# Spreading two blocks' head outputs to partitions: one set of four 64-column products at the end in place of two sets of 32

## The chip, the cores and the metric

The kernel runs on one core of a Trainium2 chip. The metric is the device time of one execution in microseconds (us), as the median of several runs; each profile is one further execution. All runs quoted here are fast: none is over 1.5% above the fastest run of its kernel. The "granted clock" is the share of PE's full clock that the trace shows as granted to it. "PE" is the matrix engine, "PEld" its weight loads, "DVE" the vector engine, "ACT" the scalar engine, "SP" the engine that issues most DMA transfers.

## The reference

Two independent attention layers decode one token each; their two output rows of 512 are concatenated.

```python
# block A: 32 heads, 32768 keys each, head size 128
q = (x @ wq).reshape(heads)
p = softmax(q @ k_cache.T * 128 ** -0.5)
a = concat_heads(p @ v_cache) @ wo          # wo: 4096 x 512
# block B: 32 query heads, 8 key/value heads, only the last 4096 keys
b = ...same...                               # own x, wq, caches, wo
return concatenate([a, b])
```

Block A reads 32 x (8.39 MB of K + 8.39 MB of V) in bf16; block B reads 16.8 MB of caches, and each block has a `wq` and a `wo` of 4.19 MB. Everything is read once.

## The kernel before

Block B runs first, in straight code; then a loop over block A's 32 heads; then both output projections. SP issues each load as soon as PE has finished with the buffer (`self.free`): there are three K buffers of 4.19 MB, of which a head of A uses two, and one V buffer of 8.39 MB. The weight `wo` of each block comes last, A's in six pieces of falling size, so that little work remains behind the last one.

```python
    def plan(self):
        ...
            self.emit_PV("B", g)
        self.emit_spread("B")                      # <- the change touches this
        for g in range(NQH):                       # NQH = 32 heads of A
            self.load_k(g, 1 if 0 < g < NQH - 1 else 2)
            self.load_v(g)
            ...
        for n in ("B", "A"):
            for part in range(len(self.WO_CUTS[n]) - 1):
                self.load_wo(n, part)              # A: rows 0:11, 11:19, 19:25, 25:29, 29:31, 31:32
        self.emit_spread("A")                      # <- and this
        self.emit_proj()                           # B's 32 products, then A's, piece by piece
```

At the end of a block its head outputs lie in tile `G` of PSUM (the memory that PE writes its products to) as 32 rows (heads) by 128 columns, with the softmax sum beside them. The projection needs them with the 4096 values spread over 128 partitions, 32 columns each. Four small products with a 0/1 matrix (`spread`) do that:

```python
    def emit_spread(self, name):
        p2 = self.G[:, 448:480] if name == "B" else self.T[0]
        ri = self.op("dve", lambda v: v.reciprocal(t["rinv"][:, :], ps[0:32, DH:DH + 1]), self.gath)
        ob = self.op("dve", lambda v: v.tensor_scalar_mul(t["ob"][:, :], ps[0:32, 0:DH], t["rinv"][:, :]), ri)
        def mm(e):
            for dq in range(4):
                inst = e.matmul(p2[:, 0:32], lhsT=self.spread[:, 128 * dq:128 * dq + 128],
                                rhs=t["ob"][:, 32 * dq:32 * dq + 32], start=(dq == 0), stop=(dq == 3), ...)
            return inst
        o = self.op("pe", mm, ob, self.k_sel)
        t["ozop"] = self.op("dve", lambda v: v.tensor_copy(t["oz"][:, :], p2[:, 0:32]), o)   # the cast
    def proj_part(self, name, part, out):
        ...
        deps = (self.wosem[name][part], 16), self.c[name]["ozop"]    # weight piece landed, cast done
        return self.op("pe", mm, *deps)
```

Of the kernel before, what the change touches and what calls it, by code (L numbers as in the profile page):

```python
# [3 lines left out]
BF16 = mybir.dt.bfloat16  # L4
# [5 lines left out]
DH = 128  # L10
# [43 lines left out]
class _Kernel:  # L54
# [120 lines left out]
    def emit(self, eng):  # L175
# [22 lines left out]
        def body(e):  # L198
# [17 lines left out]
            for k, it in enumerate(need):  # L216
                cur, plan = {}, []
                for n in it:
                    w = []
                    for name, (sem, val) in n.items():  # L220
                        if name not in sems:
                            continue
                        rel = val - start[name] - step[name] * k
                        if rel > cur.get(name, 0):
                            cur[name] = rel
                            w.append((name, rel))
                    plan.append(sorted(w))
                plans.append(plan)
# [40 lines left out]
    def alloc(self):  # L269
        nc = self.nc  # L270
        sb = nc.alloc_sbuf_tensor
        self.kbuf = sb("kbuf", [128, 3 * HALF * DH], BF16, align_bytes=4096)
        self.vbuf = sb("vbuf", [128, 2 * HALF * DH], BF16, align_bytes=4096)
        self.kt = [sb(f"kt{i}", [128, 1024], BF16) for i in range(NKT)]
        self.psb = sb("psb", [128, 512], BF16)
        self.ptsb = sb("ptsb", [128, 512], BF16)
        self.ident = sb("ident", [128, 128], BF16)
        self.ones = sb("ones", [128, 128], BF16)
        self.e32 = sb("e32", [128, 32], F32)
        self.spread = sb("spread", [32, 4 * 129], BF16)  # L280
        self.tr = {k: sb(f"tr_{k}", [128, 32], F32) for k in ("in", "a")}
        self.rows64 = sb("rows64", [128, 64], F32)
        self.nscale = sb("nscale", [1, 128], F32)
        self.m4 = sb("m4", [1, 128], F32)
        self.out_sb = sb("out_sb", [1, 512], BF16)
        self.c = {}
        for name, d in self.X.items():
            HG = d["HG"]
            self.c[name] = dict(
                x=sb(f"x_{name}", [128, 12], BF16),  # L290
                oc=[sb(f"oc_{name}{i}", [128, DH + 1], F32) for i in range(2 if name == "B" else 1)],
                b=sb(f"b_{name}", [128, 32], F32),
                cm=sb(f"cm_{name}", [128, 32], F32),
                mr=sb(f"mr_{name}", [1, HG], F32),
                nb=sb(f"nb_{name}", [128, 2], F32),
                hot=sb(f"hot_{name}", [128, d["nb"]], F32),
                lh=sb(f"lh_{name}", [128, HG], F32),
                hsel=sb(f"hsel_{name}", [128, 64], F32),
                rinv=sb(f"rinv_{name}", [32, 1], F32),
                ob=sb(f"ob_{name}", [32, DH], BF16),  # L300
                oz=sb(f"oz_{name}", [128, 32], BF16),
            )

        self.qz = sb("qz", [128, 32 * self.X["B"]["NKVH"] + 64], BF16)
        self.qa = sb("qa", [128, NQH], BF16)
        self.qrow = sb("qrow", [128, 512], BF16)
        self.qw = sb("qw", [128, 64], BF16)
        self.hw = sb("hw", [128, 32], F32)
        ps = nc.alloc_psum_tensor
        self.S = ps("psS", [128, 512], F32)  # L310
        self.T = [ps(f"psT{i}", [128, 512], F32) for i in range(NT)]
        self.PT = ps("psPT", [128, 512], F32)
        self.ACC = ps("psACC", [128, 512], F32)
        self.G = ps("psG", [128, 512], F32)
        s = nc.alloc_semaphore
        self.ksem = [s(f"ksem{i}") for i in range(2)]
        self.vsem = [s(f"vsem{i}") for i in range(2)]
        self.xsem = {n: s(f"xsem_{n}") for n in self.X}
        self.wosem = {n: [s(f"wosem_{n}{i}") for i in range(len(self.WO_CUTS[n]) - 1)] for n in self.X}
        self.outsem = {n: s(f"outsem_{n}") for n in self.X}  # L320
# [72 lines left out]
    def plan(self):  # L393
        self.lsem = {"k": self.ksem, "v": self.vsem}
        self.fill = {w: [0, 0] for w in "kv"}
        self.free = {"k": [None] * 3, "v": [None] * 2}
        self.nbatch = 0
        self.copies = []
        self.pending = []
        self.psread = self.ptread = self.sread = self.accread = None  # L400
        self.gath = self.qcopy = self.hcopy = self.qread = None
        self.constants()
        a, b = self.X["A"], self.X["B"]

        self.load_wq("B")
        self.load_b("k", 0)
        self.load_wq("A")
        self.load_b("k", 1)
        self.emit_qproj("B")
        self.emit_unit("B", 0)  # L410
        self.emit_qproj("A")
        self.emit_stats("B", 0)
        self.emit_unit("B", 1, {1: lambda: self.emit_PT("B", 0)})
        self.emit_stats("B", 1)
        for g in range(2):
            if g == 1:
                self.emit_PT("B", g)
            self.load_b("v", g)
            self.emit_PV("B", g)
        self.emit_spread("B")  # L420

        for g in range(NQH):
            self.loop = {"pe": g, "dve": g // 2}
            self.load_k(g, 1 if 0 < g < NQH - 1 else 2)
            self.load_v(g)
            self.emit_qcopy(g)
            self.emit_unit("A", g)
            self.emit_stats("A", g)
            self.emit_PT("A", g)
            self.emit_PV("A", g)  # L430
        self.loop = {}
        for n in ("B", "A"):
            for part in range(len(self.WO_CUTS[n]) - 1):
                self.load_wo(n, part)
        self.emit_spread("A")
        self.emit_proj()

    def constants(self):
# [244 lines left out]
            self.G[0:32, c0 + c:c0 + c2], lhsT=win, rhs=t["oc"][g % len(t["oc"])][:, c:c2], start=False, stop=True,  # L683
            skip_group_check=True), *(self.accread, self.sread, self.hcopy if name == "A" else self.k_sel), to="dve")

    def emit_spread(self, name):

        t = self.c[name]
        c0 = self.GCOL[name]
        ps = self.G[:, c0:c0 + DH + 1]  # L690
        p2 = self.G[:, 448:480] if name == "B" else self.T[0]
        ri = self.op("dve", lambda v: v.reciprocal(t["rinv"][:, :], ps[0:32, DH:DH + 1]), self.gath)
        ob = self.op("dve", lambda v: v.tensor_scalar_mul(t["ob"][:, :], ps[0:32, 0:DH], t["rinv"][:, :]), ri)
        def mm(e):
            inst = None
            for dq in range(4):
                inst = e.matmul(p2[:, 0:32], lhsT=self.spread[:, 128 * dq:128 * dq + 128], rhs=t["ob"][:, 32 * dq:32 * dq + 32],
                                start=(dq == 0), stop=(dq == 3), skip_group_check=True)
            return inst
        o = self.op("pe", mm, ob, self.k_sel)  # L700
        t["ozop"] = self.op("dve", lambda v: v.tensor_copy(t["oz"][:, :], p2[:, 0:32]), o)

    def proj_part(self, name, part, out):

        a0, a1 = self.WO_CUTS[name][part:part + 2]
        oz, wo = self.c[name]["oz"], self.kbuf[:, HALF * DH * self.wo_third(name):]
        def mm(e):
            inst = None
            for a in range(a0, a1):
                inst = out(e, oz[:, a:a + 1], wo[:, 512 * a:512 * a + 512], a) or inst  # L710
            return inst
        deps = (self.wosem[name][part], 16), self.c[name]["ozop"]
        return self.op("pe", mm, *deps)

    def halves(self, e, bank, lhsT, rhs, begin, end, only=(0, 1)):
# [31 lines left out]
    def emit_proj(self):  # L747

        for part in range(2):
            o = self.emit_proj_b(part)  # L750
        o = self.sum_strips(o)
        self.op("sp", lambda e: e.dma_start(self.out[0, :, 512:1024], self.qrow[0:1, :]).then_inc(self.outsem["B"], 16), o)
        for part in range(len(self.WO_CUTS["A"]) - 1):
            self.proj_part("A", part, lambda e, lhsT, rhs, a: self.halves(e, self.PT, lhsT, rhs, a == 0, False)
                           if a < 31 else None)
        oz, wo = self.c["A"]["oz"], self.kbuf[:, HALF * DH * self.wo_third("A"):]
        done = []
        for i in range(2):
            o = self.op("pe", lambda e, i=i: self.halves(e, self.PT, oz[:, 31:32], wo[:, 512 * 31:512 * 32], False, True, (i,)),
                        (self.wosem["A"][-1], 16), self.c["A"]["ozop"])  # L760
            done.append(self.store(self.PT, i, o))
        self.op("sp", lambda e: e.dma_start(self.out[0, :, 0:512], self.out_sb[:, :]).then_inc(self.outsem["A"], 16), *done)

# [26 lines left out]
```

## Time and profile before

| | before |
|---|---|
| time, median of the first 3 runs | 1322.05 us (1322.04 to 1322.24) |
| span of the profiled run | 1320.8 us |
| moved by DMA | 570.59 MB, 432 GB/s over the span |
| PE, DVE busy | 73%, 57% |
| PE's waits for the next K load | 154.2 us in 31 waits |

These lines of the page give the span, the engines' busy time and share, the DMA engines' busy share in 40 slices (9 is 90% or more), and the packets, MB and share of two DMA queues.

```profile
span 1320.8 us, 28798 instructions
...
PE 968.0 (73%) x13248; PEld 677.4 (51%) x13248; DVE 753.3 (57%) x1342; ACT 56.4 (4%) x170; POOL 2.7 (0%) x22
...
DMA  9999999999999999999999999999999999999998
...
q1 hardware_dynamic: 13060, 570.43, 99.9%
q8 instruction: 8, 0.13, 0.0%
```

The DMA row has no slice under 9 before the last, and queue 1, which carries caches and weights, fills 99.9% of the engines' time. The kernel is therefore as long as its bytes take, plus a start and a tail. The Trainium skill's page "DMA: Bandwidth & Descriptors", section "Specifications", states 435 GB/s as the fabric ceiling into SBUF; the windows view of this trace has 434 GB/s over 170 to 600 us and over 600 to 1100 us, which agrees. Queue 8 carries instructions: 8 packets.

The two places that the change touches, in the timeline: start us, length us, engine, line, operation, output<-inputs, shape, count, and in brackets how long the engine had been idle and what ended that. First the gap between the blocks:

```profile
69.44 0.15 DVE L692 RECIPROCAL rinv_B<-psG 32x1 f32<-32x1 f32 x1 [0.50 <-PE psG L682]
69.63 0.34 DVE L693 TENSOR_SCALAR ob_B<-psG,rinv_B 32x128 bf16<-32x128 f32 x1
...
70.03 0.26 PE L697 MATMUL psG<-ob_B,spread 32*128 32x32 bf16 x4 [0.62 <-DVE ob_B L693]
70.32 0.19 DVE L701 CAST oz_B<-psG 128x32 bf16<-128x32 f32 x1 [0.35 <-PE psG L697]
...
72.48 1.78 PE L552 MATMUL psT<-ident,kbuf 128*128 128x128 bf16 x15 [2.19 <-DMA kbuf<-in_A_k_cache_dram]
```

B's four products take 0.26 us on PE (line 697), its cast 0.19 us on DVE (line 701), and PE then has nothing to do until A's first K half lands: 2.19 us idle before the transposes of head 0 at 72.48.

Second, the end:

```profile
1310.51 0.34 DVE L693 TENSOR_SCALAR ob_A<-psG,rinv_A 32x128 bf16<-32x128 f32 x1
...
1311.06 0.25 PE L697 MATMUL psT<-ob_A,spread 32*128 32x32 bf16 x4 [0.78 <-DVE ob_A L693]
...
1311.24 1.90 PE L730 MATMUL psS<-kbuf,oz_B 128*1 128x512 bf16 x32
1311.35 0.19 DVE L701 CAST oz_A<-psT 128x32 bf16<-128x32 f32 x1 [0.50 <-PE psT L697]
...
1312.97 1.37 PE L718 MATMUL psPT<-kbuf,oz_A 128*1 128x256 bf16 x22
...
1314.82 1.04 PE L718 MATMUL psPT<-kbuf,oz_A 128*1 128x256 bf16 x16 [0.48 <-DMA kbuf<-in_A_wo_dram]
...
1316.67 0.32 SPq L752 DMA_DIRECT2D out_dram<-qrow  x1
...
1316.73 0.82 PE L718 MATMUL psPT<-kbuf,oz_A 128*1 128x256 bf16 x12 [0.87 <-DMA kbuf<-in_A_wo_dram]
...
1317.97 1.21 PE L718 MATMUL psPT<-kbuf,oz_A 128*1 128x256 bf16 x14 [0.42 <-DMA kbuf<-in_A_wo_dram]
...
1319.20 0.41 DVE L725 CAST out_sb<-psPT 1x256 bf16<-1x256 f32 x1 [2.56 <-PE psPT L718]
...
1319.70 0.25 SPq L762 DMA_DIRECT2D out_dram<-out_sb  x1
```

Here line 697 is A's spread, line 701 A's cast, line 730 B's 32 projection products, and line 718 A's projection. B's products do not wait for A's cast: they start at 1311.24, before it. Each of the last three rows of line 718 waited for a piece of A's weight (0.48, 0.87 and 0.42 us). The two SPq lines are the output stores, B's at 1316.67 and A's at 1319.70.

The chain of work that ended last (start us, us, what) says the same from behind:

```profile
1288.46 29.46 DMA kbuf<-in_A_wo_dram
...
1317.97 1.22 PE psPT L718 x13
...
1319.20 0.41 DVE out_sb L725
```

A load of 29.46 us, counted from its issue to its landing and so with its wait behind earlier loads in the queue, then 1.22 us of products, then the copy of the result.

### The profile page before, as it was taken

The numbers are of one execution on the slowest core, as the hardware profiler recorded it, in microseconds if no ns is written. First come the engines' busy times: TensorE is split into PE (matmuls) and PEld (weight loads), VectorE is DVE, ScalarE is ACT, GpSimd is POOL, SyncE is SP. The second block draws the span as 40 slices with busy tenths as digits, with TensorE's granted clock in tenths as the row PEclk, the third lists the DMA queues.
The fourth block names the chain that finished last, engine by engine and source line by source line (L and its number), as shares of the span: only waits on it lengthen the run. The fifth ranks groups of instructions, "written<-read, shape, count | busy, mean of one in ns | idle before, by whom it ended". The sixth has DMA issues, their size and how long they took to land. (4 is left out here: it accounts for less than half of the span.)

```text
span 1320.8 us, 28798 instructions
## 1 busy us (share of the span) xinstructions
PE 968.0 (73%) x13248; PEld 677.4 (51%) x13248; DVE 753.3 (57%) x1342; ACT 56.4 (4%) x170; POOL 2.7 (0%) x22
## 2 busy tenths in 40 slices
PE   4675678777667877777787767778776767877687
PEld 3453445555444555444455544455554445555454
DVE  3563556665455666545566654566655546665564
ACT  0000000000000000000000000000000000000000
POOL 0000000000000000000000000000000000000000
PEclk8886888887788888778988887898888789888888
DMA  9999999999999999999999999999999999999998
GB/s 404 434 435 432 441 431 435 437 431 435 435 435 437 431 435 439 429 437 437 429 437 439 429 435 439 429 435 439 429 439 437 427 441 435 429 439 435 429 439 371
DMA packets 13359, 570.59 MB, mean 432 GB/s; under 512 B 1570, under 2 KB 1700, under 8 KB 2084
## 3 DMA queue, kind: packets, MB, share of 16 engines
q1 hardware_dynamic: 13060, 570.43, 99.9%
q8 instruction: 8, 0.13, 0.0%
q10 hardware_dynamic: 288, 0.00, 0.0%
q14 instruction: 3, 0.02, 0.0%
HBM read 570.43 MB, written 0.00 MB: 432 GB/s over the span
## 5 line engine op out<-in xcount | busy, mean ns | idle before, releaser
L556 DVE COPY kt<-psT 128x1024 bf16<-128x1024 bf16 x1056 | 656.2, 684 | 238.1 <-PE psT L552 236.3
L552 PE MATMUL psT<-ident,kbuf 128*128 128x128 bf16 x8448 | 582.3, 235 | 167.8 <-DMA kbuf<-in_A_k_cache_dram 154.2
L552 PEld LDWEIGHTS psT<-ident,kbuf 128*128 128x128 bf16 x8448 | 542.7, 107 | 260.0 <-DMA kbuf<-in_A_k_cache_dram 162.3
L655 PE MATMUL psACC<-vbuf,ptsb 128*4 128x512 bf16 (+1 forms) x2112 | 185.4, 527 | 22.8 <-ACT ptsb L630 22.0
L575 PE MATMUL psS<-kt,qw 128*32 128x512 bf16 x2048 | 158.3, 386 | 14.7 <-DVE kt L556 14.7
L669 DVE TENSOR_SCALAR oc_A<-psACC,hot_A 128x128 f32<-128x128 f32 x32 | 11.2, 351 | 249.9 <-PE psG L682 249.9
L655 PEld LDWEIGHTS psACC<-vbuf,ptsb 128*4 128x4 bf16 (+1 forms) x2112 | 59.4, 111 | 139.1 <-issue 91.0
L603 ACT ACTIVATE psb<-psS,nb_A 128x512 bf16<-128x512 f32 x32 | 22.0, 687 | 1168.0 <-DVE nb_A L602 1168.0
L575 PEld LDWEIGHTS psS<-kt,qw 128*32 128x32 bf16 x2048 | 34.1, 95 | 57.4 <-DVE kt L556 30.6
L682 PE MATMUL psG<-oc_A,hw 128*32 128x128 f32 (+1 forms) x128 | 19.3, 227 | 52.3 <-DVE oc_A L671 52.3
L682 PEld LDWEIGHTS psG<-oc_A,hw 128*32 128x32 f32 x128 | 11.4, 109 | 62.5 <-DVE oc_A L671 55.0
L627 PE MATMUL psPT<-ident,psb 128*128 128x128 bf16 x136 | 18.0, 275 | 34.0 <-ACT psb L603 34.0
L671 DVE SCALAR_TENSOR_TENSOR oc_A<-psACC,hot_A,oc_A 128x128 f32<-128x128 f32 x96 | 33.7, 351 | 3.4
L592 DVE TENSOR_REDUCE tr_in<-psS 128x1 f32<-128x512 f32 x34 | 23.5, 692 | 17.8 <-PE psS L575 17.8
L627 PEld LDWEIGHTS psPT<-ident,psb 128*128 128x128 bf16 x136 | 10.2, 117 | 37.0 <-ACT psb L603 36.7
L596 PE MATMUL psACC<-rows,tr_in 128*1 128x64 f32 x64 | 8.8, 220 | 25.6 <-DVE tr_in L592 25.6
L630 ACT ACTIVATE ptsb<-psPT 128x512 bf16<-128x512 bf16 x34 | 20.3, 597 | 31.1 <-PE psPT L627 31.1
L596 PEld LDWEIGHTS psACC<-rows,tr_in 128*1 128x1 f32 x64 | 2.7, 81 | 35.7 <-DVE tr_in L592 35.7
L600 PE MATMUL psACC<-mr_A,nscale 1*128 1x1 f32 x64 | 12.3, 259 | 9.8 <-DVE mr_A L599 9.8
L600 PEld LDWEIGHTS psACC<-mr_A,nscale 1*128 1x128 f32 x64 | 9.6, 186 | 15.8 <-DVE mr_A L599 15.8
L602 DVE COPY nb_A<-psACC 128x1 f32<-128x1 f32 x32 | 5.1, 158 | 15.2 <-PE psACC L600 15.2
L599 DVE TENSOR_REDUCE mr_A<-psACC 1x1 f32<-1x64 f32 x32 | 6.8, 213 | 11.8 <-PE psACC L596 11.8
(78 smaller groups left out, 71.7 us busy)
## 6 DMA issues: line engine op xcount, KB each, us to landing
kbuf<-in_A_k_cache_dram SPq DMA_DIRECT2D x4, 4096.0 KB, 22.6
kbuf<-in_B_k_cache_dram SPq DMA_DIRECT2D x2, 4096.0 KB, 31.7
vbuf<-in_B_v_cache_dram SPq DMA_DIRECT2D x2, 4096.0 KB, 25.1
vbuf<-in_B_wq_dram SPq DMA_DIRECT2D x1, 4096.0 KB, 12.4
vbuf<-in_A_wq_dram SPq DMA_DIRECT2D x1, 4096.0 KB, 32.0
kbuf<-in_B_wo_dram SPq DMA_DIRECT2D x2, 2048.0 KB, 32.2
kbuf<-in_A_wo_dram SPq DMA_DIRECT2D x1, 1408.0 KB, 25.2
kbuf<-in_A_wo_dram SPq DMA_DIRECT2D x1, 1024.0 KB, 27.3
```

The costliest lines, as they stand in the source:

```text
L552: inst = e.transpose(T[:, 128 * k:128 * k + 128], src[:, DH * k:DH * k + DH], self.ident[:, :])
L556: self.copies.append(self.op("dve", lambda v: v.tensor_copy(KT[:, :], T[:, :]), o, to="pe"))
L575: inst = e.matmul(self.S[32 * c:32 * c + 32, :], lhsT=win, rhs=self.kt[(bb + c // 2) % NKT][:, 512 * (c % 2):512 * (c % 2) + 512], start=b ...
L592: o = dve(lambda v: v.reduce_max(tr["in"][:, 0:1], self.S[:, :], axis=AXX), self.sdone, self.k_pool, to="pe" if name == "A" else None)
L596: o = self.op("pe", lambda e: e.matmul(self.ACC[0:1, 0:64], lhsT=tr["in"][:, 0:1], rhs=self.rows64[:, :], start=True, stop=True, skip_grou ...
L600: o = self.op("pe", lambda e: e.matmul(self.ACC[:, 64:65], lhsT=self.nscale[:, :], rhs=t["mr"][0:1, :], start=True, stop=True, skip_group_ ...
L603: self.sread = self.op("act", lambda s: s.activation(out=self.psb[:, :], in_=self.S[:, :], func=ACTF.Exp, bias=t["nb"][:, k:k + 1], scale= ...
L627: inst = e.transpose(PT[:, 128 * jj:128 * jj + 128], self.psb[:, 128 * jj:128 * jj + 128], self.ident[:, :])
L630: self.ptread = self.op("act", lambda s: s.activation(out=self.ptsb[:, :], in_=PT[:, 0:512], func=ACTF.Copy), self.psread, to="pe")
L655: inst = e.matmul(acc[32 * c:32 * c + rows, 0:512], lhsT=lhsT, rhs=rhs, start=begin, stop=end, tile_position=(0, 32 * c), skip_group_check ...
L671: o = self.op("dve", lambda v, src=src, hot=hot: v.scalar_tensor_tensor(out=oc, in0=src, scalar=hot, in1=oc, op0=ALU.mult, op1=ALU.add), p ...
L682: return self.op("pe", lambda e: e.matmul(self.G[0:32, c0 + c:c0 + c2], lhsT=win, rhs=t["oc"][g % len(t["oc"])][:, c:c2], start=False, sto ...
```

## The change

Its intent is to save one set of four products and one cast: block B keeps only its normalisation behind the block, into one half of a shared tile `ob`, and at the end one set of four products of 64 columns spreads both blocks' outputs, with one cast of 64 columns.

```diff
@@ plan
-        self.emit_spread("B")
+        self.emit_norm("B")
 ...
-        self.emit_spread("A")
+        self.emit_spread()
         self.emit_proj()
@@
+    def emit_norm(self, name):        # reciprocal and scaling, as before, into ob[:, 128*n:128*n+128]
+    def emit_spread(self):
+        ob, p2 = self.ob, self.T[0]
+        o = self.emit_norm("A")
         def mm(e):
             for dq in range(4):
-                inst = e.matmul(p2[:, 0:32], ..., rhs=t["ob"][:, 32 * dq:32 * dq + 32], ...)
+                inst = e.matmul(p2[:, 0:64], ...,
+                                rhs=ob[:, :].rearrange("p (n x) -> p n x", n=2)[:, :, 32 * dq:32 * dq + 32], ...)
-        o = self.op("pe", mm, ob, self.k_sel)
-        t["ozop"] = self.op("dve", lambda v: v.tensor_copy(t["oz"][:, :], p2[:, 0:32]), o)
+        o = self.op("pe", mm, o, self.k_sel)
+        self.ozop = self.op("dve", lambda v: v.tensor_copy(self.oz[:, :], p2[:, 0:64]), o)
@@ proj_part (and the last row's products)
-        deps = (self.wosem[name][part], 16), self.c[name]["ozop"]
+        deps = (self.wosem[name][part], 16), self.ozop
```

The last line is the price: B's projection now waits for the shared cast, which comes after A's last head.

More of the change, by code (lines that the diff above doesn't have):

```diff
@@ L284, in alloc @@
         self.m4 = sb("m4", [1, 128], F32)
+        self.ob = sb("ob", [32, 2 * DH], BF16)
+        self.oz = sb("oz", [128, 64], BF16)
         self.out_sb = sb("out_sb", [1, 512], BF16)
@@ L299, in alloc @@
                 rinv=sb(f"rinv_{name}", [32, 1], F32),
-                ob=sb(f"ob_{name}", [32, DH], BF16),
-                oz=sb(f"oz_{name}", [128, 32], BF16),
             )
@@ L684, in emit_gather @@
             skip_group_check=True), *(self.accread, self.sread, self.hcopy if name == "A" else self.k_sel), to="dve")
-    def emit_spread(self, name):
-        t = self.c[name]
-        c0 = self.GCOL[name]
-        ps = self.G[:, c0:c0 + DH + 1]
-        p2 = self.G[:, 448:480] if name == "B" else self.T[0]
-        ri = self.op("dve", lambda v: v.reciprocal(t["rinv"][:, :], ps[0:32, DH:DH + 1]), self.gath)
-        ob = self.op("dve", lambda v: v.tensor_scalar_mul(t["ob"][:, :], ps[0:32, 0:DH], t["rinv"][:, :]), ri)
+    def emit_norm(self, name):
+        t, c0, n = self.c[name], self.GCOL[name], list(self.X).index(name)
+        ri = self.op("dve", lambda v: v.reciprocal(t["rinv"][:, :], self.G[0:32, c0 + DH:c0 + DH + 1]), self.gath)
+        return self.op("dve", lambda v: v.tensor_scalar_mul(
+            self.ob[:, DH * n:DH * n + DH], self.G[0:32, c0:c0 + DH], t["rinv"][:, :]), ri)
+    def emit_spread(self):
+        ob, p2 = self.ob, self.T[0]
+        o = self.emit_norm("A")
         def mm(e):
@@ L696, in mm @@
             for dq in range(4):
-                inst = e.matmul(p2[:, 0:32], lhsT=self.spread[:, 128 * dq:128 * dq + 128], rhs=t["ob"][:, 32 * dq:32 * dq + 32],
+                inst = e.matmul(p2[:, 0:64], lhsT=self.spread[:, 128 * dq:128 * dq + 128],
+                                rhs=ob[:, :].rearrange("p (n x) -> p n x", n=2)[:, :, 32 * dq:32 * dq + 32],
                                 start=(dq == 0), stop=(dq == 3), skip_group_check=True)
             return inst
-        o = self.op("pe", mm, ob, self.k_sel)
-        t["ozop"] = self.op("dve", lambda v: v.tensor_copy(t["oz"][:, :], p2[:, 0:32]), o)
+        o = self.op("pe", mm, o, self.k_sel)
+        self.ozop = self.op("dve", lambda v: v.tensor_copy(self.oz[:, :], p2[:, 0:64]), o)
+        for n, name in enumerate(self.X):
+            self.c[name]["oz"] = self.oz[:, 32 * n:32 * n + 32]
     def proj_part(self, name, part, out):
@@ L759, in emit_proj @@
             o = self.op("pe", lambda e, i=i: self.halves(e, self.PT, oz[:, 31:32], wo[:, 512 * 31:512 * 32], False, True, (i,)),
-                        (self.wosem["A"][-1], 16), self.c["A"]["ozop"])
+                        (self.wosem["A"][-1], 16), self.ozop)
             done.append(self.store(self.PT, i, o))
```

## The prediction

> **What bounds the kernel now.** The bytes it reads. The page shows 570.59 MB of DMA packets in 1320.8 us, the 16 DMA engines 99.9% busy on the queue of caches and weights, and about 432 GB/s in nearly all 40 slices; the windows view gives 434 GB/s over 170 to 600 us and 600 to 1100 us. The Trainium skill's page "DMA: Bandwidth & Descriptors", section "Specifications", gives 435 GB/s as the fabric ceiling into SBUF; this trace runs at it. PE is busy 73%, DVE 57%; the waits view shows PE waiting 154 us in 31 waits for the next K load, some 5 us to spare per head. The chain of waits ends in 29.46 us of DMA for the last pieces of A's output weight (landed at 1317.92), 1.22 us of the last products, 0.41 us of output copy, then the store.
>
> **What the change removes, adds, moves** (durations from the timeline).
> - After block B, at 70.03 us, go: four products of 32 columns (0.26 us on PE), PE's wait before them (0.62 us), one DVE cast (0.19 us). Reciprocal and scaling (0.15 + 0.34 us) stay. PE then waits for A's first K load, landing at about 72.4 us (2.19 us of idle). The gain falls into that wait and is worth nothing: PE starts the loop at the same time, and no load is issued earlier.
> - At the end, at 1311.06 us: the products and the cast are 64 columns wide instead of 32. Before they took 0.25 and 0.19 us, which look like mostly fixed cost; my estimate is under 0.1 us more for both together.
> - What moves: B's 32 products with its output weight started at 1311.24, right behind the spread, before the cast (1311.35 to 1311.54). Now they need the shared cast, so they start at about 1311.6 to 1311.7, an estimated 0.35 to 0.5 us later. They take 1.90 us; A's first 11 rows follow, ending near 1314.8 instead of 1314.34. PE's next pieces wait for loads at 1314.82, 1316.73 and 1317.96, with 0.48, 0.87 and 0.42 us of idle before them, so the delay is taken up before 1316.73. B's sum of strips shifts alike: its store issues near 1317.1 instead of 1316.67, still over 2 us ahead of A's at 1319.70, and DVE is free again before 1319.20.
>
> **On the critical path:** none of it. Loads, sizes, order and big-buffer positions are unchanged.
>
> **Predicted time:** 1322.0 us, 8 in 10 between 1321.2 and 1322.9. Chances: faster by over 2% 0.005, within 2% 0.99, slower by over 2% 0.005.
>
> **What would show it.** Right: the first transposes of head 0 still start at 72.4 to 72.5 us, with PE's idle before them grown from 2.2 to some 3 us; B's first product starts 0.3 to 0.5 us later; the wait for A's last weight piece still ends near 1317.9 and the chain has the same lines. Wrong: the last products no longer wait for a DMA and the end slips, or the DMA share drops in mid-run.
>
> **What would make it wrong.** PE's and DVE's programs get shorter before their loops, so the loops' code sits elsewhere; if instruction fetch stalled PE by more than the 5 us of slack per head, loads would be issued late. A different DMA rate in that run: 0.1% is 1.3 us, more than all that the change touches. The later store of B's half could delay the final store, if they queue behind each other.

## The result and the profile after

| | before | after |
|---|---|---|
| median, 6 runs each | 1322.05 us (1321.99 to 1323.73) | 1322.43 us (1322.37 to 1322.52) |
| ratio after to before, 95% interval | | 1.0001 (0.9988 to 1.0014) |
| span of the profiled run | 1320.8 us | 1320.6 us |

A ratio here is the mean time of one kernel's fast runs over that of the other's of the same rounds, so it is not quite the ratio of the medians. The page after:

```profile
span 1320.6 us, 28789 instructions
...
DMA  9999999999999999999999999999999999999998
...
q8 instruction: 8, 0.13, 0.0%
```

The DMA row and the instruction queue are unchanged. The gap between the blocks:

```profile
69.96 0.16 DVE L689 RECIPROCAL rinv_B<-psG 32x1 f32<-32x1 f32 x1 [0.73 <-PE psG L682]
70.15 0.34 DVE L690 TENSOR_SCALAR ob<-psG,rinv_B 32x128 bf16<-32x128 f32 x1
...
72.31 2.00 PE L552 MATMUL psT<-ident,kbuf 128*128 128x128 bf16 x17 [2.39 <-DMA kbuf<-in_A_k_cache_dram]
```

B's products and its cast are gone, and head 0 starts at 72.31 instead of 72.48, still released by the K load. What was removed became waiting. In this run B's last gather also happened to be slower (it ended at 69.92 rather than 69.41), so the idle time reads 2.39 us; in the second profile of the same kernel it is 3.38 us.

The end:

```profile
1308.10 0.34 DVE L690 TENSOR_SCALAR ob<-psG,rinv_A 32x128 bf16<-32x128 f32 x1
...
1308.65 0.28 PE L700 MATMUL psT<-ob,spread 32*128 32x64 bf16 x4 [0.78 <-DVE ob L690]
1308.97 0.23 DVE L705 CAST oz<-psT 128x64 bf16<-128x64 f32 x1 [0.53 <-PE psT L700]
...
1309.34 1.90 PE L736 MATMUL psS<-kbuf,oz 128*1 128x512 bf16 x32 [0.41 <-DVE oz L705]
...
1312.17 1.36 PE L724 MATMUL psPT<-kbuf,oz 128*1 128x256 bf16 x22 [0.93 <-DMA kbuf<-in_A_wo_dram]
...
1314.62 4.35 PE L724 MATMUL psPT<-kbuf,oz 128*1 128x256 bf16 x42 [1.08 <-DMA kbuf<-in_A_wo_dram]
1314.76 0.32 SPq L758 DMA_DIRECT2D out_dram<-qrow  x1
...
1319.49 0.25 SPq L768 DMA_DIRECT2D out_dram<-out_sb  x1
```

The four products of 64 columns take 0.28 us against 0.25, and the cast 0.23 us against 0.19: together 0.07 us more. The Trainium skill's page "TensorE: Matmul & The Clock Gate", section "Back-to-back issue gap", gives the same cycle count to all products of 1 to 64 columns; the trace agrees as far as it resolves: sets of four 32-column products took 0.25 to 0.28 us in these profiles, the 64-column set 0.28 (0.38 to 0.39 where `end_chain4` ran it at half clock). B's first product starts 0.90 us after the end of the normalisation (1308.10 + 0.34 to 1309.34), where it was 0.39 us before (1310.51 + 0.34 to 1311.24). So the delay that the change adds is 0.51 us. Behind it A's products still wait for their weights: 0.93 us before the first piece, 1.08 us before the second.

Two things in this profile look different without being due to the change. The last head ended some 2.4 us earlier, and from about 1314.7 us PE ran at half clock: the windows view (us, PE, PEld, DVE, ACT and POOL busy with counts, granted clock, DMA share, GB/s) has

```profile
1316.00:1317.00 1.00, 0.95 (x12) 0.32 (x8) 0.00 (x0) 0.00 (x0) 0.00 (x0) 0.50 0.95 375
```

with a granted clock of 0.50, where it was 1.00 before. So the chain that ended last looks different too:

```profile
1285.48 30.99 DMA kbuf<-in_A_wo_dram
...
1316.52 2.46 PE psPT L724 x17
...
1319.00 0.41 DVE out_sb L731
```

It hangs on an earlier weight piece (landed at 1316.47) and 2.46 us of slower products, and still ends within 0.2 us of where it did. In the second profile of the changed kernel, whose clock was full there, the chain is the old one: the piece lands at 1317.80, then 1.22 us of products:

```profile
1287.81 29.99 DMA kbuf<-in_A_wo_dram
...
1317.85 1.22 PE psPT L724 x13
```

The moment at which the last head ends moves from run to run by far more than the 0.51 us of the change: A's normalisation ended at 1310.85 us in the profile before, at 1308.44 and 1310.17 in the two of the changed kernel, and at 1308.96 and 1309.98 in `wait_only` and `remove_only` below. The prediction was worked out from the latest of these five, and so from the one with the least room at the end.

### The profile page after: what moved, and what is told of

Read it like the earlier page. It is cut to its first block, busy times and chain, and to the rows that moved or that the text cites. A ratio compares the mean times of both kernels' runs of the same rounds, so it can differ in the third digit from the quotient of the medians.

```text
span 1320.6 us, 28789 instructions
## 1 busy us (share of the span) xinstructions
PE 965.7 (73%) x13244; PEld 674.4 (51%) x13244; DVE 752.1 (57%) x1341; ACT 56.4 (4%) x170; POOL 2.7 (0%) x22
## 5 line engine op out<-in xcount | busy, mean ns | idle before, releaser
L682 PE MATMUL psG<-oc_A,hw 128*32 128x128 f32 (+1 forms) x128 | 19.3, 227 | 52.3 <-DVE oc_A L671 52.3
```

The source lines that it names most:

```text
L682: return self.op("pe", lambda e: e.matmul(self.G[0:32, c0 + c:c0 + c2], lhsT=win, rhs=t["oc"][g % len(t["oc"])][:, c:c2], start=False, sto ...
```

## The experiments

The theories:

- **Theory 1**: the bytes set the time. The gain between the blocks falls into a wait for a load, and the delay at the end into waits for the last weight pieces.
- **Rival 1**: the delay at the end costs; it is the 0.38 us between the two medians.
- **Rival 2**: gain and loss are both real and cancel.
- **Rival 3**: not the bytes but PE's and DVE's work per head is the limit.
- **Rival 4**: PE time between the blocks counts in full; the change gained little only because it removed little.

### The changed kernel again, and each half of the change alone

`after_again` is the changed kernel without edits. `wait_only` adds to the kernel before only the new wait:

```diff
-        deps = (self.wosem[name][part], 16), self.c[name]["ozop"]
+        deps = (self.wosem[name][part], 16), self.c[name]["ozop"], self.c["A"]["ozop"]
```

`remove_only` moves B's four products and cast to the end but keeps them as a set of their own in front of A's:

```diff
-        self.emit_spread("B")
+        self.emit_norm("B")            # reciprocal and scaling only
 ...
+        self.emit_spread("B")          # B's own four products and cast
+        self.emit_norm("A")
         self.emit_spread("A")
```

> The changed kernel once more, five rounds. Theory 1 (both ends of the change fall into waits for loads): ratio to the kernel before 1.0000 within 0.0005, so within about 0.7 us. Rival 1 (the 0.38 us between the two medians of the first measurement is a real cost at the end of the kernel): 0.3 to 0.5 us longer again, in every round.

> The kernel before with one thing done alone: B's products with its output weight also wait for A's cast; the two sets of four products stay where they were. Theory 1: B's first product starts after A's cast, 0.3 to 0.5 us later behind A's normalisation than before, and the time is the same within 0.5 us because the last pieces of A's weight land later. Rival 1: 0.3 to 0.5 us longer, all of the 0.38 us. Rival 2 (the change is neutral because a gain after block B and a loss at the end cancel): longer by the delay, 0.3 to 0.5 us.

> The kernel before with the other half done alone: B's four products and its cast move from behind block B to the end, as a set of their own in front of A's, so B's projection does not wait for A's cast. Theory 1: same within 0.5 us; PE's idle before head 0's first transposes grows from 2.2 to between 2.4 and 3.2 us and they start at the same time. Rival 2 (gain and loss cancel): 0.5 to 1.0 us shorter, the 0.26 us of products, 0.62 us of wait and 0.19 us of cast.

| run (5 rounds; before in the same rounds: 1322.23 us) | median | ratio, 95% interval |
|---|---|---|
| after_again | 1322.55 us (1322.43 to 1323.01) | 1.0003 (0.9989 to 1.0017) |
| wait_only | 1322.35 us (1322.13 to 1322.53) | 1.0000 (0.9987 to 1.0014) |
| remove_only | 1322.10 us (1322.05 to 1322.51) | 0.9999 (0.9986 to 1.0013) |

In `wait_only` B's first product starts 0.89 us after A's normalisation, as in the changed kernel, and its median is 0.12 us above before. PE's clock was even halved there for B's products (3.58 us instead of 1.90), and yet the last pieces of A's weight were still waited for:

```profile
1309.85 3.58 PE L730 MATMUL psS<-kbuf,oz_B 128*1 128x512 bf16 x32 [0.38 <-DVE oz_A L701]
...
1317.93 1.21 PE L718 MATMUL psPT<-kbuf,oz_A 128*1 128x256 bf16 x14 [0.40 <-DMA kbuf<-in_A_wo_dram]
```

In `remove_only` PE's idle before head 0 is 2.58 us and head 0 starts at 72.52 instead of 72.48:

```profile
72.52 1.78 PE L554 MATMUL psT<-ident,kbuf 128*128 128x128 bf16 x15 [2.58 <-DMA kbuf<-in_A_k_cache_dram]
```

Rival 2 needed 0.5 to 1.0 us less there. The 95% interval (about 1.8 us to either side) could not exclude that, but the five runs lie within about 0.5 us, as those of before do, and their medians are 0.13 us apart, and head 0 did not start earlier; on this evidence rival 2 falls. Rival 1 is not confirmed by `wait_only`; the small offset of the changed kernel did come back (0.32 us) and is taken up at the end of this section.

### How much room is there at the end?

`end_chain4` and `end_chain12` are the changed kernel with its four products and cast repeated 4 and 12 more times in a chain:

```diff
+        for _ in range(5):             # 13 in end_chain12
+            o = self.op("pe", mm, o, self.k_sel)
+            o = self.ozop = self.op("dve", ...tensor_copy(self.oz[:, :], p2[:, 0:64]), o)
```

> The changed kernel with its four products and cast done 4 more times in a chain at the end, each waiting for the other, so that both projections start later by 4 times about 0.69 us (0.28 us products, 0.23 us cast and the gaps), 2.8 us. Theory 1: the room at the end is the last landing near 1317.9 us less the work behind the cast (1.9 us for B and about 4 us for A at full clock), which leaves 1 to 3.5 us, so the time grows by 0 to 1.5 us. Rival 1 (a delay at the end counts in full, as the 0.4 us of the change did): 2.8 us longer.

> The same chain 12 more times: 8.3 us later. Theory 1: more than the room, so 4.5 to 7 us longer than the kernel before, and the last products no longer wait for a load. Rival 1: 8.3 us longer. If the time did not move at all, the end would not be where the kernel ends, and theory 1's account of the tail would be wrong too.

Before in the same rounds: 1322.13 us. `end_chain4`: 1323.17 us (1322.32 to 1324.07), ratio 1.0007 (0.9994 to 1.0021). `end_chain12`: 1330.03 us (1329.32 to 1330.43), ratio 1.0058 (1.0043 to 1.0074).

In its profile the 4-fold chain put off the shared cast by 2.84 us (its end moved from 1310.06 to 1312.90), and the median grew by 1.0 us, with runs from 0.2 to 1.9 us above the median of before and an interval that includes 1. The chain that ended last no longer has a DMA near its end (two of its pieces):

```profile
1313.04 3.35 PE psS L737 x24
...
1319.18 0.68 DVE qrow L747
```

It runs from B's products, slow at half clock (3.35 us for 24 of them), through B's sum on DVE. (Its program is longer and fetches a ninth packet of instructions, but only after the last weight packets had ended, so not in their way.) The 12-fold chain put the cast off by 8.07 us and cost 7.9 us, against the 4.5 to 7 us expected. The estimate had taken 1.9 us for B's 32 products, from the trace before; they took 3.58 us in this one. So the end has room for the change's 0.51 us, and by the medians for some 1.8 of 2.8 us. In `end_chain12`, where PE ran at half clock behind the cast, only about 0.2 us of 8.07 was taken up. The kernel does end there, and the room is small and not the same in every run.

### How much room is there between the blocks?

`gap_chain12` and `gap_chain40` are the kernel before with B's four products and cast repeated 12 and 40 more times in a chain behind block B:

```diff
+        for _ in range(13 if name == "B" else 1):      # 41 in gap_chain40
+            o = self.op("pe", mm, o, self.k_sel)
+            o = t["ozop"] = self.op("dve", ...tensor_copy(t["oz"][:, :], p2[:, 0:32]), o)
```

> The kernel before with the four products and the cast behind block B done 12 more times in a chain, about 0.57 us each, 6.9 us; 2 us of it fall into PE's wait for A's first K load. Theory 1: head 0 starts about 5 us late, its K is free later and the next load is issued late, but the queue still holds head 0's V (landing near 100 us, 16 us after that issue), so the time is the same within 0.5 us. Rival 4 (work on PE between the blocks counts in full, and the change gained little only because it removed little): 5 to 7 us longer.

> The same chain 40 more times, about 23 us, 21 of them past PE's wait. Theory 1: head 0's second K half is freed near 105 us instead of 84, after head 0's V has landed near 100 us, so the DMA queue runs dry for 5 to 9 us and the time grows by 4 to 12 us, less than the delay. Rival 4: 21 to 23 us longer.

Before in the same rounds: 1322.13 us. `gap_chain40`: 1332.71 us (1332.00 to 1334.44), ratio 1.0077 (1.0062 to 1.0093). Head 0 started at 93.69 us, 21.2 us late, and 10.6 us of that came out at the end. The windows view shows where they were lost:

```profile
100.00:105.00 5.00, 5.00 (x86) 3.92 (x83) 4.95 (x10) 0.00 (x0) 0.00 (x0) 1.00 0.02 3
...
125.00:130.00 5.00, 4.79 (x54) 1.66 (x46) 0.13 (x1) 0.00 (x0) 0.00 (x0) 0.61 0.05 16
```

The DMA engines moved 3 and 16 GB/s in these two stretches: the queue was empty because PE had not yet freed the buffers for the next loads (head 1's K was issued at 104.80 instead of 84.19, its V at 129.82 instead of 107.52). This is as theory 1 had it, and not rival 4: half of the delay was free. (This kernel, too, fetched a packet of instructions at its end, from 1330.03 us on, but its last chain runs through PE's products from 1327.00 us and not through the pieces that were still to land.)

`gap_chain12`: 1323.39 us (1323.17 to 1323.61), ratio 1.0009 (0.9994 to 1.0024). This is 1.3 us longer, and neither theory had it: theory 1 said within 0.5 us, rival 4 said 5 to 7. Head 0 started at 77.73 us, 5.25 us late, but head 1 started at 120.80, where it was 120.85 before, and every K load up to 1241 us released PE within 0.2 us of its time before. The loss came in the last microseconds: the piece of A's weight that ends the chain landed at 1318.93 instead of 1317.92.

What differed there is in the trace's DMA records: one more fetch of instructions by DMA, a packet of 16 KB that took 0.96 us, 1314.60 us after the first packet of the first load. (A fetch of 8 KB, 0.31 us, fell 1312.04 us after it.) The kernel before has no 16 KB fetch between 108 us and the end of its span (the next one starts 1.5 us after it). The chain had added 96 instructions to PE's program. Two runs part the delay from the fetch. `gap_dve18` makes a delay as long with 18 more copies of B's scaling on DVE, and `pad_pe48` adds as many instructions to PE as `gap_chain12` but makes nothing wait:

```diff
 gap_dve18
+        ob = ri
+        for _ in range(19 if name == "B" else 1):
+            ob = self.op("dve", ...tensor_scalar_mul(t["ob"][:, :], ps[0:32, 0:DH], t["rinv"][:, :]), ob)
 pad_pe48
+        for _ in range(12 if name == "B" else 0):
+            self.op("pe", mm, ob, self.k_sel)
```

> The kernel before with a delay behind block B as long as in the 12-fold chain, made of 18 more copies of one scaling on DVE (about 0.38 us each, 6.9 us), which adds 18 instructions to DVE and none to PE; the 12-fold chain added 96 to PE. That run was 1.2 us longer, with every K load up to 584 us landing when it did before, and with one more fetch of instructions by DMA (16 KB, 0.96 us, at 1314.6 us) amid the last weight pieces. Theory F (the fetch cost it, not the delay): head 0 starts late, near 77.5 us, and the time is the same within 0.5 us. Rival 4 (the delay cost it): about 1.2 us longer again.

> The kernel before with 48 more products behind block B, 12 sets of the same four, not waiting for anything but the first: 96 more instructions on PE as in the 12-fold chain, but under 3 us of time, nearly all of it in PE's wait for A's first K load. Theory F: a ninth fetch of 16 KB falls among the last weight pieces, near 1314 us, and the time grows by 0.9 to 1.3 us although head 0 starts at most 1 us later. Rival 4: head 0 starts at 72.5 to 73.5 us, so the time is the same within 0.3 us.

Before in the same rounds: 1322.03 us. `gap_dve18`: 1322.27 us (1322.08 to 1322.51), ratio 1.0002 (0.9985 to 1.0018). Head 0 started at 77.52 us, 5.0 us late, with no cost that the runs resolve (the medians are 0.24 us apart). Its instruction queue, and the products of A's piece that had waited until 1316.73 before:

```profile
q8 instruction: 8, 0.13, 0.0%
```

```profile
1316.84 0.82 PE L720 MATMUL psPT<-kbuf,oz_A 128*1 128x256 bf16 x12 [0.84 <-DMA kbuf<-in_A_wo_dram]
```

`pad_pe48`: 1323.81 us (1323.18 to 1324.06), ratio 1.0012 (0.9995 to 1.0028). Head 0 started at 72.67 us. The same two lines:

```profile
q8 instruction: 9, 0.15, 0.0%
```

```profile
1318.20 0.82 PE L720 MATMUL psPT<-kbuf,oz_A 128*1 128x256 bf16 x12 [2.15 <-DMA kbuf<-in_A_wo_dram]
```

There is a ninth instruction packet (0.96 us, 1315.06 us after the first load's first packet), and the same products started at 1318.20 instead of 1316.84. So a delay of 5 us between the blocks is free within the noise, and instructions that nobody waits for cost 1.8 us when their fetch falls among the last weight pieces. Theory F's sign and place are borne out; its size was not: the profiled landing moved by 1.46 us (1319.38 against 1317.92), more than the packet's own 0.96 us and more than the 0.9 to 1.3 us expected. The trace's DMA records give most of the rest. The fetch ran from 1316.08 to 1317.04 us of the span; the 6 KB weight packet that starts as it ends took 0.65 us, where the median of such packets is 0.23; and in each of the later pieces 8 of the 128 packets, the share of one of 16 DMA engines, land one after the other behind all the rest. So 0.96 + 0.42 = 1.38 us of the 1.46 are seen. That these packets run on one engine, the one that carried the fetch, is an inference from this pattern: the records do not name the engine. Behind the last landing the products of `pad_pe48` also took 1.66 us instead of 1.22. Each interval taken alone includes 1; the eight runs of the two kernels whose ninth packet fell among the last weight pieces all lie above all runs of before of their rounds.

The changed kernel has 8 instruction packets, like the one before, so none of this happened to it.

### Do the bytes set the time?

`half_v` leaves out half of one head's V, `eighth_v` the same number of bytes in four heads (results wrong):

```diff
-        self.load(self.vbuf[:, :], self.kv_src("v", "A", g)[:, 0, :], ...)
+        w = HALF * DH * (1 if g == 15 else 2)                                  # half_v
+        w = HALF * DH * 2 * (7 if g in (4, 11, 18, 25) else 8) // 8            # eighth_v
+        self.load(self.vbuf[:, 0:w], self.kv_src("v", "A", g)[:, 0, 0:w], ...)
```

> The kernel before, but head 15 of block A loads only half of its V, 4.19 MB less (its result is wrong on purpose: it uses the other half of head 14's). No instruction of PE, DVE or ACT changes. Theory 1 (the bytes set the time): 4.19 MB at the measured 434 GB/s is 9.7 us, so 1312.4 us, between 9 and 10.5 us shorter. Rival 3 (the chain of PE and DVE work per head sets the time): within 2 us of before.

`half_v`: 1318.91 us (1318.04 to 1319.34) against 1322.23 us, ratio 0.9976 (0.9960 to 0.9991). It is 3.3 us shorter, not 9.7: a miss for theory 1, and for rival 3 as well. The windows view around the cut:

```profile
670.00:675.00 5.00, 5.00 (x86) 3.94 (x84) 5.00 (x9) 0.00 (x0) 0.00 (x0) 1.00 0.59 197
675.00:680.00 5.00, 5.00 (x86) 3.95 (x84) 5.00 (x9) 0.00 (x0) 0.00 (x0) 1.00 0.73 315
```

The rate fell to 197 and 315 GB/s. In the kernel before, head 16's K is issued at 672.44 us. By an estimate, head 15's V lands at 681.0 (head 16's K released PE at 700.37, less 8.39 MB at 434 GB/s, 19.3 us). So the next load is queued 8.6 us ahead, and a single cut of 9.7 us outruns this lead: the queue runs empty until PE frees a buffer. The lead alone would leave 1.1 us empty. In the trace of `half_v` it was 3.2 us: the last packet of V ended at 671.05, head 16's K was issued only at 673.29, 0.85 us later than before, and its first packet started at 674.26, 0.97 us after its issue. At 434 GB/s those two windows lost 4.1 us (5 x (1 - 197/434) + 5 x (1 - 315/434)), and the one from 695 to 700 us, at 341 GB/s, another 1.1. The span of this profile is 4.1 us shorter than before, so 5.6 us of the 9.7 are missing; about 0.4 of them have no place. The next run was to tell this from rival 3:

> The kernel before with the same 4.19 MB left out as in the half-V run, but as one eighth of V in each of four heads far apart (4, 11, 18 and 25; wrong on purpose). In the half-V run the next K load was issued 8.6 us before head 15's V would have landed in full, so 9.7 us saved in one place ran the DMA queue dry for some 4 us. Theory 1 as now stated (the bytes set the time as long as the queue holds a next load): each cut is worth 2.4 us, less than that lead, nothing runs dry, and all 9.7 us show: 9 to 10.2 us shorter. Rival 3 as now stated (per head, PE and DVE are as close to the limit as the loads, so only part of any saving in bytes shows): 3 to 5 us shorter, as in the half-V run.

`eighth_v`: 1312.68 us (1312.32 to 1313.25) against 1322.03 us, ratio 0.9928 (0.9912 to 0.9945). The same 4.19 MB, cut in four places, brought 9.35 us of the 9.7. Theory 1 holds in the amended form: bytes set the time wherever the queue holds the next load in time.

### The 0.3 to 0.4 us that stay open

The changed kernel's median lay 0.38 and 0.32 us above before in two sittings. In its two profiles the span is not longer (1320.6 and 1320.7 against 1320.8 us). The time less the span is 1.74 and 1.76 us, where `wait_only`, `remove_only`, `half_v`, `gap_chain12` and `gap_dve18` have 1.33 to 1.35; others have other values (`end_chain4` 1.67, `eighth_v` 2.04, the profile of before 2.36). The record has the span of nearly every run (to 0.1 us), not only of the profiled ones, and says more: time less span is 1.68 to 1.77 us in all 11 runs of the changed kernel and 1.31 to 1.37 us in the 9 runs of before beside `after_again`, while the spans of these runs overlap (1320.6 to 1321.3 against 1320.7 to 1321.2). So the offset lies outside the span. A last run put B's four products back behind block B, unused, in the changed kernel:

```diff
+        self.op("pe", mm, nb, self.k_sel)     # four products of ob[:, 128:256] into G[:, 448:480]
```

> The changed kernel with block B's four products of 32 columns put back behind block B, their result unused: PE's program is as long as before, and the end is as in the changed kernel. It is for the 0.3 to 0.4 us by which the changed kernel's median was above the one before in both sittings, although its profiled spans were not longer (1320.6 and 1320.7 against 1320.8 us); profiled time less span was 1.7 to 1.8 us for it and 1.3 us for five of the other kernels. Theory F2 (that offset lies outside the span and goes with the length of PE's program): the offset is gone, within 0.15 us of the kernel before, and time less span is near 1.3 us. Rival 1 (it is the later start of B's projection at the end): 0.3 to 0.4 us longer than before again. Either is far under the 0.1% that the interval resolves, so the medians can only point.

`after_pad4`: 1322.63 us (1322.50 to 1322.75) against 1322.21 us, ratio 1.0002 (0.9988 to 1.0016). The offset stayed, and so did the 1.76 us of time less span, so theory F2 falls. Rival 1 named this number, but `wait_only` has the same late start without the offset, and rival 1's cost would have to lie inside the span, where there is none; so it falls as well. What makes these 0.03% outside the span stays open; no interval of the ratios separates them from nothing.

## Why the prediction was right

- **The number.** Predicted: 1322.0 us; measured: 1322.43. The 0.4 us between them is the offset outside the span, which the prediction did not see coming and no run explains; inside the span its account holds, as follows.
- **The bound.** Predicted: the bytes. `eighth_v` shows it: 9.7 us of bytes less gave 9.35 us less.
- **The gap between the blocks.** Predicted: worth nothing. `remove_only` moved the median by -0.13 us, head 0 kept its start, and even 5.0 us more of delay there (`gap_dve18`) was free.
- **The wider products and cast.** Predicted: under 0.1 us more. Measured: 0.07 us.
- **The delay of B's projection.** Predicted: 0.35 to 0.5 us, measured 0.51 us, just over the range. It is the sum of 0.30 us to the end of the old cast (1311.24 to 1311.54), 0.07 us for the wider set and 0.14 us from the cast's end to the first product, and the prediction does not say how it split its range, so which of the three it put too small is not known.
- **The end.** Predicted: the delay is taken up by waits for weights. `wait_only` shows it, with the wait for the last piece still 0.40 us (0.42 before). The account was narrower than it looked: from the same profile the room seemed to be 1 to 3.5 us, and it depends on the clock that PE is granted in the last 10 us. With four chain steps, 1.0 us of 2.84 us came through by the medians. That the profile it was read from had the latest end of the last head was luck, on the safe side.
- **Chain with the same lines.** Right in the second profile of the changed kernel; in the first the half clock replaced the last wait.
- **The named risks.** "5 us of slack per head" was the wrong measure: what protects the DMA is how early the next load is queued, by estimate 8.6 us at head 16's K, and more behind block B, where 5 us late was free and 21.2 us late cost 10.6. The risk from instruction fetch was real, but not in the loop, as the prediction had it: it lay among the last weight pieces. The change did not meet it.

## What to carry to other kernels

In a kernel limited by its bytes, ask of each saved instruction what its engine does next: if it waits for a load, the saving becomes waiting, and what is left for compute to shorten is the stretch behind the last landing (no run here tried that). Measure room by adding known delays rather than by reading idle times, since the clock and the lead of the load queue both change it. Removing bytes also pays only as far as the next loads are already queued, and a longer program can cost time at the end by its own fetches.

## What the Trainium skill lacked or had wrong

- "Runtime: NRT & Kernel Launch", section "Instruction fetch mechanics", calls the cost of crossing a 16 KiB boundary "mostly hidden". Here such a fetch took 0.88 to 0.97 us in most cases, and with one among the last weight loads of a kernel whose DMA is full, the time grew by 1.3 us (`gap_chain12`) and 1.8 us (`pad_pe48`).
- "DMA: Bandwidth & Descriptors", section "Specifications", lists about 358 GB/s per core for HBM beside the 435 GB/s ceiling. The figure is a stack's bandwidth divided by its two cores, and the table does not say when it binds: this kernel, on one core, moved 434 GB/s in steady state.
- No page that was read says how far ahead loads have to be queued for a saving in bytes to show: 4.19 MB less in one place gave 3.3 us, in four places 9.35 us.
- No page that was read explains the 0.4 us by which time less span differs between kernels (1.31 to 1.37 us in the runs of before beside `after_again`, 1.68 to 1.77 us in all runs of the changed kernel).
